# Lightning attention into an MLP: batch 1's scores ahead of the first MLP1 pair in wave 0, and masks ahead of batch 1's casts in wave 1

## Chip, cores and metric

The kernel runs on one core of a Trainium2 chip. The metric is the device time of one execution in microseconds. Before the change, five runs took 210.27 to 211.86 us, with a median of 211.44 us.

## What is computed

The reference takes q, k and v in float32, each of 4 batches, 8 heads, 768 positions and 64 channels, and one decay factor lam per head. Attention is linear: it goes through blocks of 64 positions and keeps a 64 x 64 state per head. Its result, tokens by (heads x channels) = 3072 x 512, goes through an MLP of 512 to 2048 to 512 with the activation h * sigmoid(1.702 h).

```python
for b in range(nb):
    sl = slice(b * block, (b + 1) * block)
    qb, kb, vb = (q[:, :, sl], k[:, :, sl], v[:, :, sl])
    intra = np.einsum('bhic,bhjc->bhij', qb, kb) * Dmask[None]
    intra = np.einsum('bhij,bhjd->bhid', intra, vb)
    inter = np.einsum('bhid,bhde->bhie', qb * lam_pow[None], kv_state)
    out[:, :, sl] = intra + inter
    kb_dec = kb * rev_pow[None]
    kv_state = lam_block[None, :, None, None] * kv_state + np.einsum('bhsd,bhse->bhde', kb_dec, vb)
...
h = x @ w_in
g = h * (1.0 / (1.0 + np.exp(-1.702 * h)))
return (g @ w_out).astype(np.float32)
```

## The kernel before

**Waves.** The work is cut into 6 waves of 512 tokens. Waves 0 and 1 (w < ND) are special: each takes two batches (wave 0 batches 0 and 1, wave 1 batches 2 and 3) with their first 256 positions; within such a wave the two batches are "batch 0" and "batch 1", the argument c. Waves 2 to 5 take 128 positions of all four batches. A wave is attention, which ends in a tile xT (channels by tokens, bf16), then MLP1 and MLP2. Attention of wave w+1 is placed among the MLP instructions of wave w.

**Attention of waves 0 and 1.** For each batch c, in this order:

- do_cast (L195) multiplies k or q by powers of lam and writes bf16: four instructions of 128 x 256 (L204). cast_v (L225) turns v to bf16, in two copies. These are the only readers of the loaded float32 tiles kf, qf and vf.
- turn_pe (L234) transposes the cast tile with eight TensorE transposes into PSUM (ps_t, L240) and copies the result to SBUF (kT, qT); the copy is by ScalarE (act_copy, L223) or VectorE (dve_copy, L220).
- d_one (L282) computes the state of the first 128 positions into PSUM (ps_kv, L277) and copies it to kv_sb on ScalarE (L285). In wave 1, start (L510) also keeps a float32 copy of it, `half`, on ScalarE (L513).
- d_scores (L253), twice: 16 matmuls each (L261), and two VectorE multiplications by the mask (sm, L265).
- d_even (L296) puts half of the state's share of the output into a PSUM tile (ps_o, L291) and lets ScalarE copy one column to `seen` (L299).
- end (L518) runs d_out (L301, masks by v, L309, and the other half of the state's share), d_state for the next positions, and the copies of the two output tiles to xT (d_x, L318), the first on ScalarE, the second on VectorE. It also writes the new state (L525 or L527).

**MLP.** mlp1 (L384) makes one 128-channel chunk of the hidden layer for all 512 tokens: 4 matmuls (L390) and a GELU on ScalarE (L392). mlp1_half (L394) makes two chunks for the 256 tokens of one batch: 8 matmuls (L402) and one GELU (L404). It lets MLP1 begin when only one batch's xT is there. mlp2 (L408) is one quarter of the sum for 128 tokens: 4 matmuls (L414); after the last quarter VectorE copies ps_out to o_sb (L418), which is stored.

**PSUM.** All PSUM tiles come from acc (L136) with one of two tags: "a" with 5 buffers, and "mm" with 3. MLP tiles ps_h and ps_out are in "mm", attention's are in "a" unless a tag is given.

**Order.** The schedule is written out by hand (manual_schedule): each engine runs its instructions in the order in which the program issues them. Wave 0's attention is a straight list (L455 to L508), with fill matmuls on zeros (L143) in the gaps. After that the MLP steps of all waves make a list main, and attention's steps are a list side of pairs (position, step). Before main step i, all side steps with a position of at most i are issued (L560). Wave 0 has main steps 0 to 30: three half steps, 12 MLP1 steps, then MLP2 from 15 on, first three token groups (0, 1, 2) side by side (15 to 26, whose last quarters are 24, 25 and 26), then group 3 (27 to 30). Wave 1 starts at 31 with eight half steps (31 to 38) and goes on with MLP1 at 39.

**Queues.** Loads of q, k and v and stores go through SyncE's queue; w_in and w_out go through GpSimd's. gate_pool (L448) makes GpSimd wait for a loaded tile by copying one element of it, so that the weights start behind it; gate_sync (L451) holds the loads of wave 1 until w_out's chunk 1 is there. Waves 2 to 5 transpose k and q by DMA (L247).

Of the kernel before, what the change touches and what calls it, by code (L numbers as in the profile page):

```python
# [24 lines left out]
def kernel(  # L25
# [13 lines left out]
    nc = tc.nc  # L39
    f32 = mybir.dt.float32  # L40
    bf16 = mybir.dt.bfloat16
    B, H, S, D = q.shape
    P = 128
    NP = H // 2
# [9 lines left out]
    EXP = mybir.ActivationFunctionType.Exp  # L54
# [10 lines left out]
    work = ctx.enter_context(tc.tile_pool(name="work", bufs=2))  # L65
# [5 lines left out]
    HF = 2  # L71
    HD = H * D

    loaded = {}
# [36 lines left out]
    A, Z = slice(0, 64), slice(64, P)  # L111
# [15 lines left out]
    i_k = const.tile([P, 1], f32)  # L127
    iota(i_k, [[0, 1]], P - 1, -1)
    i_q = const.tile([P, 1], f32)
# [9 lines left out]
    def fill(n, new=None):  # L139
        if new:  # L140
            fill_ps[0] = acc("ps_fill", shape=[P, W], tag=new)
        for _ in range(n):
            nc.tensor.matmul(fill_ps[0], zero[:, 0:P], zero, start=True, stop=True)  # L143
# [7 lines left out]
    def mk_pow(x, scale):  # L151
        nc.scalar.activation(x, ln_lam, EXP, scale=scale)
# [5 lines left out]
            mk_pow(x[:, :, a], i[:, a : a + 1])  # L158
    k_pow = const.tile([P, 2, H], f32)
    q_pow = const.tile([P, 2, H], f32)  # L160
    for x, i in ((k_pow, i_k), (q_pow, i_q)):
        nc.scalar.activation(x, ln_lam.unsqueeze(1).to_broadcast([P, 2, H]), EXP, scale=i)
    inv_pow = const.tile([P, H], f32)
    mk_pow(inv_pow, -1.0 * P)
    blk_pow = const.tile([P, NP], f32)
    for j, rows in enumerate((A, Z)):
        nc.scalar.activation(blk_pow[rows].rearrange("p (r i) -> p r i", i=2),
                             ln_lam[rows].rearrange("p (r j i) -> p r j i", i=2, j=2)[:, :, j, :], EXP, scale=1.0 * P)
    warm = const.tile([P, 1], f32)

    v_sb = [const.tile([P, B, H, D], bf16, name=f"v_sb{i}") for i in range(2)]
# [99 lines left out]
    def d_state(w, c, t, bs):  # L271
        ks, vt = cast[w, c, "k"], v_sb[w % 2]
        for p in range(NP):
            for a in range(2):
                for j, js in enumerate((A, Z)):
                    h, n0 = 4 * (p // 2) + 2 * j + p % 2, p * P + j * D
                    nc.tensor.matmul(t[js, p, :], ks[bs, a, n0 : n0 + D], vt[bs, 2 * c + a, h, :],  # L277
                                     start=((bs is A or (w, c) in kept) and p + a == 0), stop=(a == 1), skip_group_check=True)
# [3 lines left out]
    def d_one(w, c, tag="a"):  # L282
        states[w, c] = t = acc("ps_kv", shape=[P, NP, D], tag=tag)
        d_state(w, c, t, A)
        nc.scalar.copy(kv_sb[1][:, 2 * w + c], t)  # L285

    def d_inter(w, c, t, j, first):
        js, b = (A, Z)[j], 2 * w + c
# [7 lines left out]
    def d_even(w, c, tag="a"):  # L296
        whole[w, c] = acc("ps_o", tag=tag)
        d_inter(w, c, whole[w, c], 0, True)
        nc.scalar.copy(seen, whole[w, c][:, 0, 0:1])  # L299
# [18 lines left out]
    def d_x(w, c, i, t, copy):  # L318
        n0 = (2 * c + i) * P
        copy(xT[w][:, :, n0 : n0 + P], t)  # L320
# [73 lines left out]
    def mlp1_half(w, c, fc):  # L394
        if w not in g_of:
            g_of[w] = gp.tile([P, FFC, W], bf16, tag="g", name="g_sb")
        cols = slice(c * W // 2, (c + 1) * W // 2)
        h = acc("ps_h", shape=[P, 2, W // 2], tag="mm")
        for u in range(2):
            j, i = w_in_of[fc + u]  # L400
            for kc in range(KC):
                nc.tensor.matmul(h[:, u, :], w_in_sb[j][:, kc, i * P : (i + 1) * P], xT[w][:, kc, cols],  # L402
                                 start=(kc == 0), stop=(kc == KC - 1))
        nc.scalar.activation(g_of[w][:, fc : fc + 2, cols], h, GELU)  # L404
# [43 lines left out]
    def gate_pool(x):  # L448
        nc.gpsimd.tensor_copy(behind_q, x)
# [2 lines left out]
        nc.sync.dma_start(out=behind, in_=x)  # L452

    with tc.manual_schedule():
        nc.scalar.activation(warm, q_pow[:, 0, 0:1], GELU)  # L455
        fill(5)
        for g in range(2):
            do_cast(0, 0, "k", nc.vector, g)
            turn_pe(0, 0, "k", act_copy, g)
            fill(2)  # L460
        for g in range(2):
            do_cast(0, 0, "q", nc.vector, g)
            turn_pe(0, 0, "q", act_copy, g)
            fill(2 - 2 * g)
        gate_pool(loaded[0, 0, "v"][0:1, 0, 0:1])
        load_w_in(0)
        cast_v(0, 0, (act_copy, act_copy))
        d_scores(0, 0, 0)
        fill(1)
        d_scores(0, 0, 1)  # L470
        fill(3)
        for g in range(2):
            do_cast(0, 1, "k", nc.gpsimd, g)
        for j in (1, 2):
            load_w_in(j)
        d_one(0, 0, "mm")
        fill(1, "a")
        oa, oz = d_out(0, 0, ("mm", "mm"))
        nc.scalar.copy(seen, oz[:, 3, P - 1 : P])
        d_state(0, 0, states[0, 0], Z)  # L480
        fill(1)
        d_inter(0, 0, oz, 0, False)
        d_x(0, 0, 0, oa, act_copy)
        d_x(0, 0, 1, oz, act_copy)
        do_cast(0, 1, "q", nc.vector, 0)
        do_cast(0, 1, "q", nc.vector, 1)
        turn_pe(0, 1, "k", dve_copy)
        dve_copy(kv_sb[0][:, 0], states[0, 0])
        turn_pe(0, 1, "q", act_copy, 0)
        fill(2, "a")  # L490
        turn_pe(0, 1, "q", act_copy, 1)
        fill(2)
        cast_v(0, 1, (act_copy, pool_copy))
        for j in range(3, len(IN_CH)):
            load_w_in(j)
        for j in range(NCH):
            load_w_out(j)
        nc.gpsimd.affine_select(mask, mask, pattern=[[0, 1], [1, P]], channel_multiplier=-1, base=0,
                                compare_op=mybir.AluOpType.is_ge, fill=0.0)
        gate_sync(w_out_sb[1][0:1, 0, 0:2])  # L500
        load(1)
        d_scores(0, 1, 0)
        mlp1_half(0, 0, 0)
        d_scores(0, 1, 1)
        d_one(0, 1)
        fill(1, "mm")
        d_even(0, 1)
        fill(1)  # L508

        def start(w, c):  # L510
            d_one(w, c)
            kept[w, c] = work.tile([P, NP, D], f32, tag="half", name="half")
            nc.scalar.copy(kept[w, c], states[w, c])  # L513
            for pp in range(2):
                d_scores(w, c, pp)
            d_even(w, c)

        def end(w, c):  # L518
            oa, oz = d_out(w, c)
            t = acc("ps_kv", shape=[P, NP, D]) if w else states[w, c]  # L520
            d_state(w, c, t, Z)
            d_x(w, c, 0, oa, act_copy)
            d_x(w, c, 1, oz, dve_copy)
            if w:
                nc.vector.tensor_tensor(kv_sb[0][:, 2 * w + c], kept[w, c], t, op=ADD)  # L525
            else:
                nc.scalar.copy(kv_sb[0][:, 2 * w + c], t)  # L527

        def stores():
            for f in late:  # L530
                f()

        side, main = [(0, (end, 0, 1))], []
        for w in range(NW):
            n = len(main)
            main += mlp_items(w)
            e = len(main)
            x = w + 1
            if x < ND:
                for c in range(HF):  # L540
                    t, d = n + 24 + 5 * c, n + 19 + 7.5 * c
                    side += [(d, (do_cast, x, c, "k", nc.vector)), (d + 1 + 0.5 * c, (do_cast, x, c, "q", nc.vector)),
                             (d, (cast_v, x, c)),
                             (t, (turn_pe, x, c, "k", act_copy)),
                             (t + 1.5 + 0.5 * c, (turn_pe, x, c, "q", (act_copy, dve_copy)[c])),
                             (t + 3, (start, x, c)), (t + 6 - c, (end, x, c))]
            elif x < NW:
                for c in range(HF):
                    tk, tq = (n + 2.1 + 2 * c, n + 4 + c) if x == ND else (n + 4 + 2 * c, n + 5 + 2 * c)
                    side += [(tk, (do_cast, x, c, "k", nc.vector)), (tk, (turn_dma, x, c, "k")),  # L550
                             (tq, (do_cast, x, c, "q", nc.vector)), (tq, (turn_dma, x, c, "q")),
                             (n + 10 + 2 * c, (cast_v, x, c))]
                if x == ND:
                    side += [(n + 7, (stores,))]
                t = n + 16
                side += [(t, (n_two, x, 0)), (t + 4, (n_two, x, 1)), (t + 9, (n_rest, x))]
            if w + 2 < NW:
                side += [(n + (12 if w else 20), (load, w + 2))]
        side.sort(key=lambda x: x[0])
        for i, (f, *a) in enumerate(main):  # L560
            while side and side[0][0] <= i:
                _, (g, *b) = side.pop(0)
                g(*b)
            f(*a)
# [30 lines left out]
```

## Time and profile before

One execution was profiled. All times below are of it, unless said otherwise; starts count from the start of the span.

| what | value |
|---|---|
| median of five runs | 211.44 us (210.27 to 211.86) |
| profiled execution | 211.44 us |
| its span | 209.7 us |
| mean granted TensorE clock | 0.997 |
| TensorE busy, until 58 us / whole span | 54.72 / 203.0 us |
| VectorE, ScalarE, GpSimd busy | 90.5, 83.7, 24.6 us |
| first MLP2 matmul of wave 0 | 31.91 us |
| first full MLP1 matmul of wave 1 | 61.27 us |

The timeline gives, for a run of like instructions on an engine, the start, the length in us, the engine (PE is TensorE's matmuls, PEld its weight loads, DVE VectorE, ACT ScalarE, POOL GpSimd, SPq SyncE's DMA issues), the line, the operation, its output and inputs, the shape and the count; brackets give the idle time before the first of them and what ended it. The length of a TensorE run includes the modelled tail of its last matmul, so the prediction works with starts. The list of waits gives who waited for whom, the total in us, the number of times and the longest.

### The profile page before, as it was taken

The numbers are of one execution on the slowest core, as the hardware profiler recorded it, in microseconds if no ns is written. First come the engines' busy times: TensorE is split into PE (matmuls) and PEld (weight loads), VectorE is DVE, ScalarE is ACT, GpSimd is POOL, SyncE is SP. The second block draws the span as 40 slices with busy tenths as digits, with TensorE's granted clock in tenths as the row PEclk, the third lists the DMA queues.
The fourth block names the chain that finished last, engine by engine and source line by source line (L and its number), as shares of the span: only waits on it lengthen the run. The fifth ranks groups of instructions, "written<-read, shape, count | busy, mean of one in ns | idle before, by whom it ended". The sixth has DMA issues, their size and how long they took to land.

```text
span 209.7 us, 4320 instructions
## 1 busy us (share of the span) xinstructions
PE 203.0 (97%) x1837; PEld 105.8 (50%) x1837; DVE 90.5 (43%) x156; ACT 83.7 (40%) x153; POOL 24.6 (12%) x43
## 2 busy tenths in 40 slices
PE   7999999989899999999999999999999999999993
PEld 2567544556674455444455444464444454444463
DVE  1785000689990654650754730744720741100121
ACT  5965661134556103366102366012466021565000
POOL 4594000230220000300012000021000000000000
PEclk9999999999999999999999999999999999999998
DMA  5999999999849899989994379991370021100112
GB/s 168 335 229 203 194 205 285 303 289 216 191 109 164 193 250 221 240 186 161 239 239 141 101 174 209 221 269 55 98 158 0 20 84 50 50 0 3 50 54 96
DMA packets 87640, 33.82 MB, mean 161 GB/s; under 512 B 67398, under 2 KB 84678, under 8 KB 87622
## 3 DMA queue, kind: packets, MB, share of 16 engines
q1 hardware_dynamic: 82868, 29.37, 56.8%
q0 software_dynamic: 4752, 4.19, 12.7%
q8 instruction: 14, 0.23, 0.4%
q14 instruction: 4, 0.03, 0.0%
q10 hardware_dynamic: 2, 0.00, 0.0%
HBM read 27.26 MB, written 6.29 MB: 160 GB/s over the span
## 4 chain that ended last, share of the span: by engine, by line
PE 71%; DVE 0%; issue 0%
PE ps_out L414 34%; PE ps_h L390 30%; PE ps_s L328 2%; PE ps_o L378 2%; PE ps_h L402 2%; PE ps_o L365 1%; PE ps_kv L352 1%; DVE o_sb L418 0%
## 5 line engine op out<-in xcount | busy, mean ns | idle before, releaser
L414 PE MATMUL ps_out<-w_out,g_sb 128*128 128x512 bf16 (+2 forms) x416 | 86.2, 363 | 0.0
L390 PE MATMUL ps_h<-xT,w_in 128*128 128x512 bf16 x336 | 73.5, 379 | 0.0
L392 ACT ACTIVATE g_sb<-ps_h 128x512 bf16<-128x512 f32 x84 | 50.2, 597 | 45.2 <-PE ps_h L390 45.2
L414 PEld LDWEIGHTS <-g_sb 128*128 128x128 bf16 x416 | 38.1, 98 | 41.1
L390 PEld LDWEIGHTS <-w_in 128*128 128x128 bf16 x336 | 32.9, 98 | 39.2
L418 DVE COPY o_sb<-ps_out 128x512 f32<-128x512 f32 (+2 forms) x26 | 16.9, 650 | 53.6 <-PE ps_out L414 50.8
L336 DVE SCALAR_TENSOR_TENSOR sm<-ps_s,inv_pow,mask 128x512 bf16<-128x512 f32 x32 | 21.8, 743 | 31.4 <-PE ps_s L328 25.1
L217 POOL CAST v_sb<-vf 128x1024 bf16<-128x1024 f32 (+1 forms) x13 | 12.4, 961 | 112.4 <-DMA vf<-in_v_dram 100.3
L382 ACT CAST xT<-ps_o 128x512 bf16<-128x512 f32 x16 | 8.2, 599 | 37.8 <-PE ps_o L378 37.8
L204 DVE TENSOR_TENSOR ks<-kf,kd_pow 128x256 bf16<-128x256 f32 x12 | 5.1, 487 | 20.6 <-DMA kf<-in_k_dram 16.9
L402 PE MATMUL ps_h<-xT,w_in 128*128 128x256 bf16 x96 | 11.5, 273 | 0.8 <-DVE xT L220 0.8
L211 DVE TENSOR_TENSOR ks<-kf,k_pow 128x512 bf16<-128x512 f32 x16 | 11.9, 782 | 0.0
L143 PE MATMUL ps_fill<-zero 128*128 128x512 bf16 x27 | 10.3, 477 | 1.4 <-DVE zero L113 1.4
L265 DVE TENSOR_TENSOR sm<-ps_s,mask_d 128x512 bf16<-128x512 f32 x16 | 10.0, 682 | 2.7 <-PE ps_s L261 2.7
L211 DVE TENSOR_TENSOR qs<-qf,q_pow 128x512 bf16<-128x512 f32 x16 | 11.1, 733 | 0.0
L404 ACT ACTIVATE g_sb<-ps_h 128x512 bf16<-128x512 f32 x12 | 7.2, 597 | 7.4 <-PE ps_h L402 7.4
L402 PEld LDWEIGHTS <-w_in 128*128 128x128 bf16 x96 | 8.9, 98 | 2.4 <-DVE xT L220 1.1
L356 DVE SCALAR_TENSOR_TENSOR kv<-kv,blk_pow,ps_kv 128x256 bf16<-128x256 bf16 x12 | 5.0, 475 | 6.0 <-PE ps_kv L352 6.0
L223 ACT COPY kT<-ps_t 128x512 bf16<-128x512 bf16 (+1 forms) x4 | 3.1, 795 | 10.2 <-PE ps_t L240 10.2
L204 DVE TENSOR_TENSOR qs<-qf,qd_pow 128x256 bf16<-128x256 f32 x16 | 6.2, 451 | 0.1
L328 PEld LDWEIGHTS <-kT 64*128 64x128 bf16 x128 | 3.6, 94 | 3.4 <-issue 3.4
L328 PE MATMUL ps_s<-qT,kT 64*128 64x128 bf16 x128 | 5.0, 217 | 0.0
(64 smaller groups left out, 84.7 us busy)
## 6 DMA issues: line engine op xcount, KB each, us to landing
vf<-in_v_dram SPq DMA_DIRECT2D x11, 512.0 KB, 6.5
kf<-in_k_dram SPq DMA_DIRECT2D x10, 512.0 KB, 5.8
qf<-in_q_dram SPq DMA_DIRECT2D x10, 512.0 KB, 6.6
out_dram<-o_sb SPq DMA_DIRECT2D x15, 256.0 KB, 2.0
out_dram<-o_sb SPq DMA_DIRECT2D x17, 128.0 KB, 2.4
w_out<-in_moe_w_out_dram POOLq DMA_DIRECT2D x4, 512.0 KB, 15.1
w_in<-in_moe_w_in_dram POOLq DMA_DIRECT2D x3, 512.0 KB, 8.8
kf<-in_k_dram SPq DMA_DIRECT2D x4, 256.0 KB, 3.1
```

Of the source, the lines that this page charges most:

```text
L143: nc.tensor.matmul(fill_ps[0], zero[:, 0:P], zero, start=True, stop=True)
L204: eng.tensor_tensor(x.rearrange("p a (r i j d) -> p r j i a d", i=2, j=2, d=D)[:, R, j], f[:, h].rearrange("p i (a d) -> p i a d", a=2), p ...
L211: eng.tensor_tensor(x.rearrange("p b (r i j d) -> p j (b r) i d", i=2, j=2, d=D)[:, j], f.rearrange("p h (a d) -> p (h a) d", a=2).rearran ...
L217: nc.gpsimd.tensor_copy(out, in_)
L265: nc.vector.tensor_tensor(sm.rearrange("p i a s -> p i (a s)"), s2[h].rearrange("p (i a) s -> p i (a s)", i=2), mask_d.rearrange("p o a b ...
L328: nc.tensor.matmul(s2[h][:, b, :], kT[hs, (b % 2) * NP + p, :], qT[hs, (b % 2) * NP + p, :], start=True, stop=True)
L336: nc.vector.scalar_tensor_tensor(sm, s, inv_pow[:, n : n + 1], mask.to_broadcast([P, B, P]), op0=MUL, op1=MUL)
L390: nc.tensor.matmul(h, w_in_sb[j][:, kc, i * P : (i + 1) * P], xT[w][:, kc, :], start=(kc == 0), stop=(kc == KC - 1))
L392: nc.scalar.activation(g_of[w][:, fc, :], h, GELU)
L402: nc.tensor.matmul(h[:, u, :], w_in_sb[j][:, kc, i * P : (i + 1) * P], xT[w][:, kc, cols], start=(kc == 0), stop=(kc == KC - 1))
L414: nc.tensor.matmul(ps_out, g_of[w][:, fc, g * P : (g + 1) * P], w_out_sb[j][:, fc % CW, c0:c1], start=(fc == 0), stop=(fc == FFC - 1))
L418: nc.vector.tensor_copy(o, ps_out)
```

## The change

- The five ScalarE instructions that make k_pow, q_pow, inv_pow and blk_pow are issued inside the hand-written schedule, behind kd_pow and qd_pow.
- GpSimd's gate ahead of the first w_in chunk waits for the second half of q (heads 4 to 7) of batch 0, no longer for the first half of v.
- In wave 0 the first MLP1 half step (two chunks, 8 matmuls) moves from between batch 1's two d_scores to behind d_even, and one fill goes.
- The copies of d_one are a function of their own, d_keep; in wave 1, batch 1's d_one and d_keep move into the end of batch 0.
- In wave 1 batch 0's steps are placed earlier (k's transposes before step 22, no longer 24; q's 24, no longer 26; start 25, no longer 27; end 29, no longer 30), and batch 1's casts come behind batch 0's masks: k on GpSimd (24), q on VectorE (26). Both batches' v is cast on ScalarE (20 and 27), no longer on GpSimd.
- Batch 0's d_even takes a PSUM buffer of tag "mm"; batch 1's qT copy and the second copy to its xT go from VectorE to ScalarE.
- From wave 2 on, v is cast on VectorE, no longer on GpSimd.

```diff
--- before.py
+++ after.py
@@ -158,14 +158,8 @@
             mk_pow(x[:, :, a], i[:, a : a + 1])
     k_pow = const.tile([P, 2, H], f32)
     q_pow = const.tile([P, 2, H], f32)
-    for x, i in ((k_pow, i_k), (q_pow, i_q)):
-        nc.scalar.activation(x, ln_lam.unsqueeze(1).to_broadcast([P, 2, H]), EXP, scale=i)
     inv_pow = const.tile([P, H], f32)
-    mk_pow(inv_pow, -1.0 * P)
     blk_pow = const.tile([P, NP], f32)
-    for j, rows in enumerate((A, Z)):
-        nc.scalar.activation(blk_pow[rows].rearrange("p (r i) -> p r i", i=2),
-                             ln_lam[rows].rearrange("p (r j i) -> p r j i", i=2, j=2)[:, :, j, :], EXP, scale=1.0 * P)
     warm = const.tile([P, 1], f32)
 
     v_sb = [const.tile([P, B, H, D], bf16, name=f"v_sb{i}") for i in range(2)]
@@ -282,7 +276,12 @@
     def d_one(w, c, tag="a"):
         states[w, c] = t = acc("ps_kv", shape=[P, NP, D], tag=tag)
         d_state(w, c, t, A)
-        nc.scalar.copy(kv_sb[1][:, 2 * w + c], t)
+
+    def d_keep(w, c):
+        nc.scalar.copy(kv_sb[1][:, 2 * w + c], states[w, c])
+        if w:
+            kept[w, c] = work.tile([P, NP, D], f32, tag="half", name="half")
+            nc.scalar.copy(kept[w, c], states[w, c])
 
     def d_inter(w, c, t, j, first):
         js, b = (A, Z)[j], 2 * w + c
@@ -452,6 +451,12 @@
         nc.sync.dma_start(out=behind, in_=x)
 
     with tc.manual_schedule():
+        for x, i in ((k_pow, i_k), (q_pow, i_q)):
+            nc.scalar.activation(x, ln_lam.unsqueeze(1).to_broadcast([P, 2, H]), EXP, scale=i)
+        mk_pow(inv_pow, -1.0 * P)
+        for j, rows in enumerate((A, Z)):
+            nc.scalar.activation(blk_pow[rows].rearrange("p (r i) -> p r i", i=2),
+                                 ln_lam[rows].rearrange("p (r j i) -> p r j i", i=2, j=2)[:, :, j, :], EXP, scale=1.0 * P)
         nc.scalar.activation(warm, q_pow[:, 0, 0:1], GELU)
         fill(5)
         for g in range(2):
@@ -462,7 +467,7 @@
             do_cast(0, 0, "q", nc.vector, g)
             turn_pe(0, 0, "q", act_copy, g)
             fill(2 - 2 * g)
-        gate_pool(loaded[0, 0, "v"][0:1, 0, 0:1])
+        gate_pool(loaded[0, 0, "q"][0:1, 4, 0:1])
         load_w_in(0)
         cast_v(0, 0, (act_copy, act_copy))
         d_scores(0, 0, 0)
@@ -474,6 +479,7 @@
         for j in (1, 2):
             load_w_in(j)
         d_one(0, 0, "mm")
+        d_keep(0, 0)
         fill(1, "a")
         oa, oz = d_out(0, 0, ("mm", "mm"))
         nc.scalar.copy(seen, oz[:, 3, P - 1 : P])
@@ -500,31 +506,35 @@
         gate_sync(w_out_sb[1][0:1, 0, 0:2])
         load(1)
         d_scores(0, 1, 0)
-        mlp1_half(0, 0, 0)
         d_scores(0, 1, 1)
         d_one(0, 1)
+        d_keep(0, 1)
         fill(1, "mm")
         d_even(0, 1)
-        fill(1)
+        mlp1_half(0, 0, 0)
 
         def start(w, c):
-            d_one(w, c)
-            kept[w, c] = work.tile([P, NP, D], f32, tag="half", name="half")
-            nc.scalar.copy(kept[w, c], states[w, c])
+            if c == 0:
+                d_one(w, c)
+                d_keep(w, c)
             for pp in range(2):
                 d_scores(w, c, pp)
-            d_even(w, c)
+            d_even(w, c, ("mm", "a")[c])
 
         def end(w, c):
             oa, oz = d_out(w, c)
             t = acc("ps_kv", shape=[P, NP, D]) if w else states[w, c]
             d_state(w, c, t, Z)
+            if w and c == 0:
+                d_one(w, 1)
             d_x(w, c, 0, oa, act_copy)
-            d_x(w, c, 1, oz, dve_copy)
+            d_x(w, c, 1, oz, act_copy if w and c else dve_copy)
             if w:
                 nc.vector.tensor_tensor(kv_sb[0][:, 2 * w + c], kept[w, c], t, op=ADD)
             else:
                 nc.scalar.copy(kv_sb[0][:, 2 * w + c], t)
+            if w and c == 0:
+                d_keep(w, 1)
 
         def stores():
             for f in late:
@@ -537,19 +547,20 @@
             e = len(main)
             x = w + 1
             if x < ND:
-                for c in range(HF):
-                    t, d = n + 24 + 5 * c, n + 19 + 7.5 * c
-                    side += [(d, (do_cast, x, c, "k", nc.vector)), (d + 1 + 0.5 * c, (do_cast, x, c, "q", nc.vector)),
-                             (d, (cast_v, x, c)),
-                             (t, (turn_pe, x, c, "k", act_copy)),
-                             (t + 1.5 + 0.5 * c, (turn_pe, x, c, "q", (act_copy, dve_copy)[c])),
-                             (t + 3, (start, x, c)), (t + 6 - c, (end, x, c))]
+                for c, (k_at, q_at, v_at, k_turn, q_turn, s_at, e_at) in enumerate(
+                        ((19, 20, 20, 22, 23.5, 25, 28.5), (24, 26, 26.5, 28, 30.5, 32, 34))):
+                    side += [(n + k_at, (do_cast, x, c, "k", (nc.vector, nc.gpsimd)[c])),
+                             (n + q_at, (do_cast, x, c, "q", nc.vector)),
+                             (n + v_at, (cast_v, x, c, (act_copy, act_copy))),
+                             (n + k_turn, (turn_pe, x, c, "k", act_copy)),
+                             (n + q_turn, (turn_pe, x, c, "q", act_copy)),
+                             (n + s_at, (start, x, c)), (n + e_at, (end, x, c))]
             elif x < NW:
                 for c in range(HF):
                     tk, tq = (n + 2.1 + 2 * c, n + 4 + c) if x == ND else (n + 4 + 2 * c, n + 5 + 2 * c)
                     side += [(tk, (do_cast, x, c, "k", nc.vector)), (tk, (turn_dma, x, c, "k")),
                              (tq, (do_cast, x, c, "q", nc.vector)), (tq, (turn_dma, x, c, "q")),
-                             (n + 10 + 2 * c, (cast_v, x, c))]
+                             (n + 10 + 2 * c, (cast_v, x, c, (dve_copy,)))]
                 if x == ND:
                     side += [(n + 7, (stores,))]
                 t = n + 16
```

## The prediction

> **What bounds the kernel now.** I read the page first, then the chain that ended last, then who waited for whom between 30 and 62 us, then the timeline there. The page's first row:
>
> ```profile
> PE 203.0 (97%) x1837; PEld 105.8 (50%) x1837; DVE 90.5 (43%) x156; ACT 83.7 (40%) x153; POOL 24.6 (12%) x43
> ```
>
> The chain in order of time begins so, and nothing but PE follows until the last 0.3 us:
>
> ```profile
> 57.72 0.05 issue
> 57.77 3.67 PE ps_h L402 x32
> 61.44 6.91 PE ps_h L390 x32
> ```
>
> From 57.77 us on TensorE never waits, so no edit of later waves can gain, and a gain must come from before that point. What TensorE waited for from 30 to 62 us (total, times, longest):
>
> ```profile
> PE ps_h L402 <- DVE xT L220: 0.8, 1, 0.8
> PE ps_t L240 <- DVE sm L265: 0.3, 1, 0.3
> PE ps_o L291 <- ACT half L513: 0.2, 1, 0.2
> ```
>
> The timeline there (start, us long, engine, operation):
>
> ```profile
> 39.50 1.17 POOL L217 CAST v_sb<-vf 128x512 bf16<-128x512 f32 x2 [21.33 <-DMA vf<-in_v_dram]
> 40.33 1.01 ACT L223 COPY kT<-ps_t 128x1024 bf16<-128x1024 bf16 x1 [7.62 <-PE ps_t L240]
> 42.05 0.69 DVE L418 COPY o_sb<-ps_out 128x512 f32<-128x512 f32 x1 [0.17 <-PE ps_out L414]
> 42.50 1.01 ACT L223 COPY qT<-ps_t 128x1024 bf16<-128x1024 bf16 x1 [1.16 <-PE ps_t L240]
> 43.56 0.64 PE L261 MATMUL ps_s<-qT,kT 64*64 64x128 bf16 x32
> 43.97 2.25 DVE L204 TENSOR_TENSOR ks<-kf,kd_pow 128x256 bf16<-128x256 f32 x4
> 46.14 2.47 DVE L265 TENSOR_TENSOR sm<-ps_s,mask_d 128x512 bf16<-128x512 f32 x4
> 46.87 0.61 PE L240 MATMUL ps_t<-ident,ks 128*128 128x128 bf16 x8 [0.31 <-DVE sm L265]
> 57.03 0.68 DVE L220 CAST xT<-ps_o 128x512 bf16<-128x512 f32 x1
> ```
>
> Two things matter. The masks, ready to go at 44.0, run at 46.14 behind batch 1's k casts on VectorE. And TensorE waits for a mask at 46.87 not because it needs it, but because its new PSUM tile (tag "a", 5 buffers) takes the buffer of the first score tile; the wait on `half` is of this kind too. So buffers are reused strictly in turn.
>
> With starts of TensorE operations I sum its idle time in wave 1's attention, steps too small for the waits list included: 0.3 at 44.4, 0.5 at 46.87, 0.25 at 52.13, 0.2 at 52.88, 1.0 at 57.77: 2.2 us. That and some 0.5 us in wave 0 (the starts between 14.93 and 18.92 against the durations below) is all there is: 1.3% at the very most.
>
> **Start and wave 0.** The moved powers are the same five ScalarE instructions in another order. ScalarE runs without a gap from 3.83 to 10.41, its first kT copy at 7.26, so VectorE's casts may start 0.5 sooner (kd_pow comes first), but they then wait for ScalarE: 0 (0.1 gain at most). The gate on GpSimd waits for q's second half in place of v's first. v landed at 2.96 + 4.4 = 7.36; q's issue at 2.4, with a landing between 3.9 and 4.5 us as its neighbours, gives 6.3 to 6.9. So w_in's first chunk is issued some 0.8 us sooner, into DMA queues already full (345 GB/s at 9 to 10 us). It can delay batch 1's k (landing 8.9, read by GpSimd at 9.03) by up to 0.8 x half the rate = 0.4, and GpSimd's k casts end at 11.75 instead of 11.35; the transposes want them at 13.07: hidden. Later weights queue behind each other up to 34 us whatever the issue time: 0, bounds -0.3 to +0.4 for wave 1's loads.
>
> In wave 0 the MLP1 pair (0.98 us) goes behind d_even and one fill goes (0.22). ScalarE's state copy, at 16.96 behind the pair's GELU, moves to about 16.2, so d_even's wait (17.07 to 17.39) goes. What is late next:
>
> ```profile
> 15.39 2.62 DVE L265 TENSOR_TENSOR sm<-ps_s,mask_d 128x512 bf16<-128x512 f32 x4 [0.64 <-PE ps_s L261]
> 17.94 0.69 PE L309 MATMUL ps_o<-sm,v_sb 64*64 64x128 bf16 x32
> ```
>
> The masks still end at 18.01 and d_out's last quarter needs them. I walk d_scores 14.93, second scores 15.25 (second qT copy ends 15.19), d_one 15.78 (ScalarE's v cast ends 15.71), d_even 16.7, pair to 17.85, d_out to 18.36 instead of 18.43: 0.07 gained.
>
> **Wave 1, walked.** Durations: one MLP2 step (4 L414) 0.863 ((39.68-31.91)/9); 8 transposes 0.45; d_one 0.30; scores 0.55; d_even 0.23; d_out 0.5, then 0.11 and d_state 0.35; half MLP1 step 0.875 (57.77 to 61.27, by 4); 0.1 more on going to half-size tiles (42.30 to 43.26). ScalarE: two v casts 1.14 (row at 9.27), kT and qT copies 1.01. VectorE: masks 2.48 from 0.46 after the scores begin (52.13, 52.59), o_sb copy 0.69. A copy's end reaches TensorE 0.05 later (43.51, 43.56); transposes reach ScalarE after 0.65 (39.68, 40.33).
>
> Step 15 at 31.84. k's transposes before step 22 at 37.88 (its casts end at 37.84, as now), q's before 24 at 40.06, d_one at 41.47 to 41.77. Now the new wait. ScalarE takes v's cast before the kT copy in its in-order queue, and v lands late (KB each, us from issue to landing, one issue at 31.62):
>
> ```profile
> vf<-in_v_dram SPq DMA_DIRECT2D x1, 512.0 KB, 7.8
> ```
>
> 39.42. Casts to 40.6, kT to 41.55, qT to 42.5, scores at 42.55: TensorE waits 0.78, and 1.0 us is still gained on the old 43.56. Masks 43.01 to 45.49. d_even is now in tag "mm" (3 buffers) between ps_out of token groups 2 and 3, so group 3's ps_out reuses group 1's buffer, whose o_sb copy is behind the masks: 45.42 to 46.11. TensorE, through steps 25 and 26 at 45.06, waits to 46.17: 1.11. Queued behind it is everything on TensorE. Before, this copy ran at 42.05 and no L414 matmul waited in the trace, so the cost is bounded by 0 and 1.11; I take the upper end, because the "a" buffers show the reuse in turn twice. The Trainium skill's "Perfetto Trace Analysis" (Optimizing Tensor Performance, Matmuls) has groups rotate through PSUM banks so that the evacuation of one lies beside the next one's matmuls; here the rotation is kept but one more tile enters it. By the row of before (no wait) the sum would be 1.1 better, by the rule's condition broken it is as walked.
>
> On: step 27 to 47.03, k's transposes to 47.48, step 28, end of batch 0 from 48.44 to 49.40, d_one of batch 1 to 49.70 (its old wait on `half` goes), steps 29, 30 to 51.43, q's transposes to 51.88, half step 31 to 52.86; qT copy 52.08 to 53.09, scores 53.14 (wait 0.28), d_even to 53.92, half steps to 55.77, d_out to 56.27 (masks end 56.08), state to 56.73, step 34 to 57.61. xT's two copies on ScalarE end at 57.66: 57.68, wait 0.07 in place of 1.0. Then 3.50 to step 39: 61.18 against 61.27 now. Wave 0's 0.07 is lost in the wait for v.
>
> **What lies off the path.** Batch 1's k casts on GpSimd: the row of wave 0 has 604 ns x 4 (2.32 us) against 418 ns on VectorE. The Trainium skill's "GPSIMD Engine Reference" (4.1 Engine selection) speaks against it: two-input elementwise work is about twice as slow there. k lands between v at 39.42 and q at 42.4; by the row the cast ends at 41.8 to 44.8, by the rule (2 x 1.43) at 42.3 to 45.3; its transposes come at 47.03. Both give 0. v's casts on VectorE from wave 2 on: no row casts SBUF to SBUF there; between 0.69 (1024 elements, L220) and 1.36 (twice L211's 0.68 for 512) each, nearer the second, since it reads f32 from SBUF too. They fall at 63 to 65.6, where VectorE idles 6.28 us before 68.77; later waves have it at 49% (80 to 110 us). Zero; without that cover up to 2.7 us a wave would stand ahead of masks. Wave 2's casts start 1.1 us later behind batch 1's masks, but without GpSimd's v casts beside them 2.12 falls to 1.28; the SyncE transposes and loads behind them keep some 3 us to the scores at 68.34.
>
> **Sum.** Stalls after 0.78+1.11+0.28+0.07 = 2.24 for 2.2 before: the old waits go, two new ones take their place. Difference -0.1 us. The profiled execution took 211.44 with a span of 209.7 (1.7 around it), equal to the median: 211.3.
>
> **Rivals.** *Stalls only change places*, 0.60: 211.3, own range 210.6 to 212.1 (v's landing +-0.3, durations +-0.4). *A new wait is not there*, 0.22: if group 3 needn't wait for group 1's copy, 1.1 less: 210.2; if v lands by 38.6, the first wait goes, 0.8 less: 210.5; with both 209.4. For it: no L414 wait now; against: reuse in turn, full queues up to v. I give it 210.3. *Slower: v later*, 0.18. v to casts, kT, qT, scores, masks, o_sb copy and ps_out is one chain without slack, so each 0.1 us of v is 0.1 us of time. The earlier w_in in front of wave 0's loads holds GpSimd's casts and so every weight behind them, w_out's chunk 1 and the gate of wave 1's loads (29.75) among these. It decides from a landing of 40.6 (1.2 later); at 40.7 it gives 212.6. Against it: 1.3 us is three times what I bound. That the edits don't do what they say isn't likely: program order is plain in each engine's rows.
>
> 0.5% (1.06 us) is about what can be told from no change. Faster by more 0.22, within 0.60, slower 0.18. The range takes the nearer part of both neighbours: 210.2 to 212.5.
>
> **What would show it.** Right: scores of batch 0 at 42.5 with TensorE waiting for ScalarE's qT; masks at 43.0; a new wait of ps_out L414 on o_sb L418 near 46; xT's wait at 57.8 under 0.2; L390 starting near 61.2. Wrong: no L414 wait, v's cast on ScalarE not near 39.5, a wait of ps_t on GpSimd's k cast, or any TensorE wait after 62.

## The result: 0.63% slower, and the profile after

The changed kernel took 211.91 us (median of 38 runs, 210.70 to 214.36) against 210.61 us for the kernel before (75 runs, 209.87 to 211.86): ratio 1.0063, 95% interval 1.0049 to 1.0077. It is slower by 1.3 us, where no change was forecast. Both the lowest time (0.83 us up) and the width of the times grew. Two of the 38 runs (214.08 and 214.36 us, at a granted clock of 0.992) are slow ones, and such runs are left out of all ratios here, though not of the medians.

The profiled execution of the changed kernel took 213.01 us with a span of 211.3. Its page has these rows for TensorE's work and for the chain that ended last. DMA and SyncE's queue now have a share of the chain, which before was TensorE alone:

```profile
PE 202.8 (96%) x1836; PEld 105.7 (50%) x1836; DVE 89.5 (42%) x158; ACT 87.2 (41%) x159; POOL 15.2 (7%) x35
...
PE 75%; DMA 14%; SPq 4%; ACT 2%; DVE 1%; POOL 1%; issue 1%; DVEq 0%
```

What TensorE waited for between 30 and 64 us (total, times, longest); lines have moved, so that L413 is mlp2's matmul, L255 the scores, L234 the transposes:

```profile
PE ps_out L413 <- DVE o_sb L417: 1.0, 1, 1.0
PE ps_s L255 <- ACT qT L217: 1.0, 2, 0.8
PE ps_t L234 <- DVE ks L198: 0.5, 2, 0.3
```

The two new waits of the prediction are there, near the sizes it gave (0.78 and 1.11). The third row was not forecast: k's transposes wait for VectorE's casts. The old waits on xT, on a mask and on `half` are gone. The timeline shows the same chain, but late:

```profile
16.47 0.62 ACT L217 CAST v_sb<-vf 128x512 bf16<-128x512 f32 x1 [1.17 <-DMA vf<-in_v_dram]
17.14 0.44 PE L271 MATMUL ps_kv<-v_sb,ks 64*64 64x64 bf16 x16 [1.37 <-ACT v_sb L217]
...
38.83 1.43 DVE L198 TENSOR_TENSOR ks<-kf,kd_pow 128x256 bf16<-128x256 f32 x4 [18.02 <-DMA kf<-in_k_dram]
39.65 0.40 PE L234 MATMUL ps_t<-ident,ks 128*128 128x128 bf16 x4 [0.26 <-DVE ks L198]
40.31 0.40 PE L234 MATMUL ps_t<-ident,ks 128*128 128x128 bf16 x4 [0.27 <-DVE ks L198]
...
41.88 1.14 ACT L217 CAST v_sb<-vf 128x512 bf16<-128x512 f32 x2 [7.91 <-DMA vf<-in_v_dram]
42.93 1.00 ACT L217 COPY kT<-ps_t 128x1024 bf16<-128x1024 bf16 x1
...
44.90 0.64 PE L255 MATMUL ps_s<-qT,kT 64*64 64x128 bf16 x32 [0.78 <-ACT qT L217]
45.35 2.48 DVE L259 TENSOR_TENSOR sm<-ps_s,mask_d 128x512 bf16<-128x512 f32 x4 [0.88 <-PE ps_s L255]
47.76 0.68 DVE L417 COPY o_sb<-ps_out 128x512 f32<-128x512 f32 x1
48.49 1.02 PE L413 MATMUL ps_out<-w_out,g_sb 128*128 128x512 bf16 x4 [1.01 <-DVE o_sb L417]
```

Wave 1's v is cast at 41.88, not 39.5; every step after it is 2.3 to 2.4 us later than walked (scores 44.90 for 42.55, masks 45.35 for 43.01, ps_out 48.49 for 46.17). In wave 0, v of batch 1 is late as well, and TensorE waits 1.37 us for its cast. So TensorE is late before it comes to v of wave 1: the first MLP2 matmul starts at 33.18 us (31.84 in the walk), k's transposes at 39.65 (37.88 in the walk). Without the 0.78 us for v the scores would still have started at 44.12. The loads are late together, not that v alone: k's first cast starts at 38.83 us, where it started at 36.41 before.

The chain that ended last, in order of time, shows how a late v in wave 0 reaches wave 1:

```profile
8.60 7.86 DMA vf<-in_v_dram
16.51 0.61 POOL v_sb L211
17.12 1.44 POOL w_in L177 x2
18.55 0.72 POOL w_out L181
19.27 12.87 DMA w_out<-in_moe_w_out_dram
32.16 0.77 SPq L451
...
34.03 7.83 DMA vf<-in_v_dram
41.88 1.14 ACT v_sb L217 x2
```

GpSimd casts half of batch 1's v ahead of its issues of the rest of w_in and of w_out; w_out's chunk 1 opens SyncE's gate (L451), and wave 1's loads start behind that. So the question was not whether the walk was right, but why the loads were late.

### The profile page after: what moved, and what is told of

Its sections match the earlier page's. It is cut to its first block, busy times and chain, and to the rows that moved or that the text cites. A ratio compares the mean times of both kernels' runs of the same rounds, so it can differ in the third digit from the quotient of the medians.

```text
span 211.3 us, 4305 instructions
## 1 busy us (share of the span) xinstructions
PE 202.8 (96%) x1836; PEld 105.7 (50%) x1836; DVE 89.5 (42%) x158; ACT 87.2 (41%) x159; POOL 15.2 (7%) x35
## 4 chain that ended last, share of the span: by engine, by line
PE 75%; DMA 14%; SPq 4%; ACT 2%; DVE 1%; POOL 1%; issue 1%; DVEq 0%
PE ps_out L413 35%; PE ps_h L389 29%; DMA vf<-in_v_dram 7%; DMA w_out<-in_moe_w_out_dram 6%; SPq L81 4%; PE ps_h L401 3%; PE ps_s L327 2%; PE ps_o L377 2%; PE ps_o L364 1%; ACT qT L217 1%; DVE sm L259 1%; PE ps_kv L351 1%; POOL w_in L177 1%; PE ps_o L308 1%; ACT v_sb L217 1%
## 5 line engine op out<-in xcount | busy, mean ns | idle before, releaser
L413 PE MATMUL ps_out<-w_out,g_sb 128*128 128x512 bf16 (+2 forms) x416 | 86.4, 363 | 1.0 <-DVE o_sb L417 1.0
L413 PEld LDWEIGHTS <-g_sb 128*128 128x128 bf16 x416 | 38.2, 98 | 42.2 <-issue 1.3
L198 DVE TENSOR_TENSOR ks<-kf,kd_pow 128x256 bf16<-128x256 f32 x8 | 2.9, 421 | 21.3 <-DMA kf<-in_k_dram 18.0
L205 DVE TENSOR_TENSOR qs<-qf,q_pow 128x512 bf16<-128x512 f32 x16 | 10.3, 684 | 0.0
L205 DVE TENSOR_TENSOR ks<-kf,k_pow 128x512 bf16<-128x512 f32 x16 | 10.3, 683 | 0.0
L217 ACT CAST v_sb<-vf 128x512 bf16<-128x512 f32 x7 | 4.0, 617 | 9.6 <-DMA vf<-in_v_dram 9.6
L198 POOL TENSOR_TENSOR ks<-kf,kd_pow 128x256 bf16<-128x256 f32 x8 | 4.7, 607 | 22.7 <-DMA kf<-in_k_dram 21.6
L217 ACT COPY qT<-ps_t 128x512 bf16<-128x512 bf16 (+1 forms) x6 | 4.4, 728 | 2.0 <-PE ps_t L234 1.8
```

The lines of the kernel that those rows point to most:

```text
L198: eng.tensor_tensor(x.rearrange("p a (r i j d) -> p r j i a d", i=2, j=2, d=D)[:, R, j], f[:, h].rearrange("p i (a d) -> p i a d", a=2), p ...
L205: eng.tensor_tensor(x.rearrange("p b (r i j d) -> p j (b r) i d", i=2, j=2, d=D)[:, j], f.rearrange("p h (a d) -> p (h a) d", a=2).rearran ...
L217: nc.scalar.copy(out, in_)
L413: nc.tensor.matmul(ps_out, g_of[w][:, fc, g * P : (g + 1) * P], w_out_sb[j][:, fc % CW, c0:c1], start=(fc == 0), stop=(fc == FFC - 1))
```

## The experiments

Each ratio is to runs of the kernel before taken beside that kernel; their median went from 210.20 to 210.66 us, so ratios compare better than medians.

| kernel | runs | lowest us | median us | ratio to before (95%) |
|---|---|---|---|---|
| 1 wave-1 part only | 18 | 210.73 | 211.43 | 1.0058 (1.0035 to 1.0081) |
| 2 changed, gate on v | 6 | 212.04 | 213.15 | 1.0122 (1.0074 to 1.0170) |
| 3 changed, powers back | 20 | 210.66 | 211.97 | 1.0073 (1.0050 to 1.0095) |
| 4 before, gate on q | 22 | 209.87 | 210.00 | 0.9983 (0.9966 to 1.0000) |
| 5 changed, batch 0's v on GpSimd | 22 | 209.79 | 211.04 | 1.0006 (0.9989 to 1.0023) |
| 6 changed, d_even in "a" | 22 | 209.51 | 210.62 | 0.9997 (0.9974 to 1.0021) |
| 7 changed, loads sooner | 6 | 211.80 | 212.49 | 1.0085 (1.0053 to 1.0117) |
| 8 before, batch 1's v on ScalarE | 22 | 209.81 | 209.87 | 0.9970 (0.9954 to 0.9985) |
| 9 both waits taken away (5 and 6) | 22 | 209.04 | 210.08 | 0.9970 (0.9950 to 0.9989) |
| 10 old order, waits taken away | 24 | 209.69 | 209.73 | 0.9969 (0.9954 to 0.9985) |
| 11 wave-0 part only | 14 | 209.70 | 210.53 | 0.9991 (0.9964 to 1.0019) |
| 12 as 9, old wave 0 | 22 | 209.17 | 210.26 | 0.9975 (0.9953 to 0.9997) |
| 13 as 12, one step later | 12 | 209.13 | 209.17 | 0.9937 (0.9916 to 0.9957) |
| 14 before, profiled again | 1 | 210.37 | | |

**1 to 4: which part, and is it the gate or the powers?** Kernel 1 is the kernel before with the wave-1 part (and the later v casts) alone.

> Only the wave-1 part and the later v casts; start and wave 0 as before. Theory A (the gate lets the first w_in chunk in front of batch 1's loads, so v of wave 0 and all weights are late): v of wave 1 lands near 39.4 again, scores of batch 0 near 42.5, ratio to before 0.997 to 1.002. Theory B (the moved powers start VectorE's casts earlier and SyncE's issues of the loads then take longer): the same here. Theory C (loads land later in some executions whatever the kernel, and only wave 1's new order without slack shows it): still 1.004 to 1.007.

Kernel 2 is the changed kernel with one line back:

```diff
-        gate_pool(loaded[0, 0, "q"][0:1, 4, 0:1])
+        gate_pool(loaded[0, 0, "v"][0:1, 0, 0:1])
```

> The changed kernel with GpSimd's gate back on v. Theory A: batch 1's v lands near 12.6 in place of 16.5, ratio to before 0.997 to 1.002. Theories B and C: as the changed kernel, 1.005 to 1.008, v near 16.

Kernel 3 puts the five powers back where they were:

```diff
     with tc.manual_schedule():
-        for x, i in ((k_pow, i_k), (q_pow, i_q)):
-            nc.scalar.activation(x, ...)
-        mk_pow(inv_pow, -1.0 * P)
...
```

> The changed kernel with the powers back in their old order. Theory B: SyncE's issue of k of batch 1 takes 1.8 us again in place of 2.7, v of batch 1 lands near 13, ratio 0.997 to 1.002. Theories A and C: 1.005 to 1.008.

Kernel 4 has nothing but the gate's line of the change.

> The kernel before with the gate on q's second half alone. Theory A: v of batch 1 later than 14, the loads of wave 1 1 to 2 us later, but the time only 0 to 0.5% longer, since the old wave-1 order has some 2.6 us between v's cast and its first reader. Theories B and C: no change, 0.998 to 1.002.

The wave-1 part alone gives the whole loss (1.0058). Theories A and B fall: with the gate back the changed kernel is still slower than before (1.0122), the gate alone costs nothing (0.9983), and with the powers back the loss stays (1.0073). Kernel 3's profile happens to be one in which wave 1's loads come as early as in the first profile of before, and it is a test of the walk:

```profile
36.48 1.44 DVE L204 TENSOR_TENSOR ks<-kf,kd_pow 128x256 bf16<-128x256 f32 x4 [17.05 <-DMA kf<-in_k_dram]
...
39.54 1.14 ACT L223 CAST v_sb<-vf 128x512 bf16<-128x512 f32 x2 [6.94 <-DMA vf<-in_v_dram]
...
42.55 0.64 PE L261 MATMUL ps_s<-qT,kT 64*64 64x128 bf16 x32 [0.69 <-ACT qT L223]
43.01 2.48 DVE L265 TENSOR_TENSOR sm<-ps_s,mask_d 128x512 bf16<-128x512 f32 x4 [0.79 <-PE ps_s L261]
...
46.15 1.02 PE L419 MATMUL ps_out<-w_out,g_sb 128*128 128x512 bf16 x4 [1.01 <-DVE o_sb L423]
...
60.92 3.40 PE L395 MATMUL ps_h<-xT,w_in 128*128 128x512 bf16 x14
```

Walked were 42.55, 43.01, 46.17 and 61.18. This execution took 210.69 us, 0.75 less than the profiled 211.44 of before. Only 0.35 of this lies ahead of wave 1's full MLP1 (60.92 against 61.27). The other 0.4 lies at the very end, behind VectorE's last output copy: from the start of that MLP1 to the end of the copy both take 145.4 us. All ten profiles of kernels with the change's wave 1 and its later v casts have this gain (the time less that start is 149.73 to 149.77 us), and the six others don't (150.11 to 150.18). Which edit brings it was not tested.

In the other profiles the loads come later. The five profiles that have the changed wave 1 with both new waits give:

| kernel | k's cast on VectorE starts, us | v's cast on ScalarE starts, us | scores start, us | time of that execution, us |
|---|---|---|---|---|
| 3 | 36.48 | 39.54 | 42.55 | 210.69 |
| 1 | 36.74 | 39.80 | 42.81 | 210.94 |
| 2 | 38.18 | 41.24 | 44.25 | 212.36 |
| 7 | 38.32 | 41.38 | 44.39 | 212.50 |
| changed | 38.83 | 41.88 | 44.90 | 213.01 |

From first to last v is 2.34 us later and the time 2.32 us longer, and the three between lie on that line within 0.03. But k is later by the same amount: v follows it by 3.05 or 3.06 us in all five, and the scores by 6.07. So this table can't tell a chain through v from one through k. The kernels below that take v out of ScalarE's way can: in three of them (5, 12 and 13) TensorE waits for k's casts, and the scores start 5.16 us behind the first of these. So k has no slack either. The lateness that k and v share goes into the time in full, and v's place ahead of kT costs 0.9 us on top (6.07 less 5.16).

**5 and 6: one wait each.** Kernel 5 takes v out of the way of ScalarE's copies, kernel 6 frees ps_out from the masks:

```diff
-                             (n + v_at, (cast_v, x, c, (act_copy, act_copy))),
+                             (n + v_at, (cast_v, x, c, ((pool_copy, pool_copy), (act_copy, act_copy))[c])),
```

> The changed kernel with wave 1's batch 0 v cast on GpSimd again, so that ScalarE's kT and qT copies no longer queue behind v. Theory D (the loss is two new waits, qT behind v 0.8 us and more when v lands late, and ps_out behind the masks 1.0 us): the scores start near 41.8, the qT wait is under 0.1, the ps_out wait stays at 1.0; 0.8 us faster than the changed kernel at its best (210.7 to 209.9) and its spread to higher times shrinks; ratio to before 0.996 to 1.001. Theory E (the loss is the extra work on ScalarE and GpSimd, not the waits): 1.005.

```diff
-            d_even(w, c, ("mm", "a")[c])
+            d_even(w, c)
```

> The changed kernel with batch 0's d_even in a PSUM buffer of tag a again. Theory D: no wait of ps_out on o_sb; instead d_even waits some 0.2 to 0.3 us for the copy half; at its best 0.8 us faster than the changed kernel (209.9), the spread stays as wide, since v is still ahead of kT; ratio 1.000 to 1.003. Theory E: 1.006.

Each brings the lowest time down, by 0.9 and 1.2 us from the changed kernel's 210.70; in kernel 6's profile no ps_out wait is left, in kernel 5's that wait stands at 0.9 and no qT wait of batch 0 is left. Theory E falls. In kernel 5 the spread did not shrink as expected: with v out of the way it is k's casts, just as late, that TensorE waits for (k first cast at 37.81, a wait of 0.5 us in all, scores at 42.97).

**7: loads sooner.** The gate of wave 1's loads waits for w_out's chunk 0:

```diff
-        gate_sync(w_out_sb[1][0:1, 0, 0:2])
+        gate_sync(w_out_sb[0][0:1, 0, 0:2])
```

> The changed kernel with the loads of wave 1 held only until w_out's chunk 0 is there. Theory D: v lands 1.5 to 2.4 us sooner, the qT wait goes (0.8), the ps_out wait of 1.0 stays, most of the spread goes; ratio 0.996 to 1.001, unless w_out's chunks 1 to 3 now come too late for MLP2, which would show as a wait of L413 on the DMA of w_out. Theory E: 1.006.

A miss. The first load was issued at 29.32 us (30.57 in the first profile of before), but v was cast at 41.38: it took 10.9 us from issue to landing, where it took 7.8 in the changed kernel's profile. Between 29 and 42 us GpSimd's queue still moved 1.13 MB through the same DMA engines; that this took v's share is likely, but no run separates it. The time follows k and v as in the table.

**8 and 14: was the profile of before a typical one?** Its v casts of batch 1 on GpSimd lay exactly on VectorE's k casts. Kernel 8 moves them to ScalarE, behind batch 0's scores:

```diff
-                             (d, (cast_v, x, c)),
+                             ((d, 28.2)[c], (cast_v, x, c, ((pool_copy, pool_copy), (act_copy, act_copy))[c])),
```

> The kernel before with wave 1's batch 1 v cast on ScalarE, behind batch 0's scores, so that it no longer lies beside VectorE's k cast. Theory F (in its profiled execution VectorE's k casts took 2.25 us beside GpSimd's v casts in place of 1.42, which made the 0.3 and 0.8 us waits; executions without that overlap are the fast ones): k casts 1.42 us, no xT wait, times from 209.9 up with fewer above 211, ratio 0.996 to 1.000. If those waits belong to the old order itself: ratio 1.000, xT's wait stays.

> The kernel before once more, for a second profile. Theory H: k of wave 1's batch 0 is first read later than the 36.41 us of the first profile, most likely at 37.5 to 38.3; batch 1's v then lands after VectorE's k casts, these take 1.42 in place of 2.25 us, there is no xT wait of 0.8, and the time is 209.9 to 210.4. If the first profile was typical: 36.4 again, 2.25, the wait of 0.8, 211.4.

Kernel 8 is 0.30% faster, and its times are narrow: 17 of 22 below 210.1. The second profile of the unchanged kernel (kernel 14) shows why the times of before vary. First two lines of the first profile, then kernel 14's timeline, then all its waits of TensorE from 30 to 64 us:

```profile
36.41 1.43 DVE L204 TENSOR_TENSOR ks<-kf,kd_pow 128x256 bf16<-128x256 f32 x4 [16.87 <-DMA kf<-in_k_dram]
...
43.99 1.62 POOL L217 CAST v_sb<-vf 128x512 bf16<-128x512 f32 x2 [3.32 <-DMA vf<-in_v_dram]
```

```profile
37.96 1.43 DVE L204 TENSOR_TENSOR ks<-kf,kd_pow 128x256 bf16<-128x256 f32 x4 [17.95 <-DMA kf<-in_k_dram]
...
44.44 1.42 DVE L204 TENSOR_TENSOR ks<-kf,kd_pow 128x256 bf16<-128x256 f32 x4
...
45.78 2.48 DVE L265 TENSOR_TENSOR sm<-ps_s,mask_d 128x512 bf16<-128x512 f32 x4
45.81 1.17 POOL L217 CAST v_sb<-vf 128x512 bf16<-128x512 f32 x2 [3.61 <-DMA vf<-in_v_dram]
```

```profile
PE ps_o L291 <- ACT half L513: 0.6, 2, 0.4
PE ps_out L414 <- issue: 0.2, 1, 0.2
```

k is first read at 37.96, 1.55 us later than in the first profile; batch 1's v then lands behind VectorE's k casts and beside the masks. The casts take 1.42 us where they took 2.25, the v casts 1.17 where they took 1.62, and the waits on a mask and on xT (0.3 and 0.8) are not there. The Trainium skill's "SBUF — State Buffer" (Who interferes with whom) says that a VectorE instruction with two SBUF inputs contends with a GpSimd instruction that reads SBUF, and one with at most one SBUF input, outside the modes in which VectorE takes two ports, does not. Both measurements agree: k casts (two inputs in SBUF) slow down, masks (one in PSUM) take 2.48 us beside the same v casts. So in the kernel before the later loads of kernel 14 gave the faster execution (210.37 against 211.44 us); in the changed kernel, every late load costs.

**9 and 10: both waits taken away, in the new and in the old order.** Kernel 9 is kernels 5 and 6 in one.

> The changed kernel with both mends: batch 0's v of wave 1 on GpSimd, and its d_even in a tag a buffer. Theory D: neither the qT wait (over 0.1) nor the ps_out wait; at its best 208.8 to 209.2, 1.5 to 1.9 us below the changed kernel's 210.7; ratio 0.993 to 0.998. If the two mends don't add, because what was hidden behind the one wait comes out (the transposes waiting for k's casts, d_one waiting for v): 209.5 at its best, ratio 0.997 to 1.001.

Its profile's waits from 0 to 66 us (a wait at the very start left out) are:

```profile
PE ps_o L290 <- ACT half L284: 0.2, 1, 0.2
PE ps_s L255 <- ACT qT L217: 0.2, 1, 0.2
```

The mends bring 1.66 us of the 2.1 that they brought one by one: 209.04 at the lowest against the changed kernel's 210.70, and 0.30% faster than before. Kernel 10 keeps the old positions:

```diff
-                    t, d = n + 24 + 5 * c, n + 19 + 7.5 * c
...
+                        ((19, 20, 20, 24, 25.5, 27, 30), (26.5, 28, 28.2, 29, 31, 32, 34))):
...
-            d_even(w, c)
+            d_even(w, c, ("mm", "a")[c])
```

> The old order of waves 0 and 1 with only those edits that take a wait away: batch 1's v on ScalarE behind batch 0's scores, d_even of batch 0 in tag mm (here the o_sb copies stand ahead of the masks), batch 1's d_one in the end of batch 0, the gate on q. Theory D and F: the 0.6 us of waits on half go and no ps_out wait comes; 209.2 at its best, tight, ratio 0.993 to 0.996. If the mm buffer costs a ps_out wait in this order too: 209.8 or more.

Half a miss: no ps_out wait came, so tag "mm" costs nothing where the o_sb copies stand ahead of the masks, but the 0.6 us did not become time. In its profile (210.73 us, near the top of its runs, which go from 209.69 to 210.93) a wait of 0.3 on qT's VectorE copy, which d_one had covered before, and 0.2 on xT stand in their place.

**11 to 13: where does the rest of the spread come from?** Kernel 11 is the kernel before with the start and wave 0 of the change, kernel 12 is kernel 9 with the old order in wave 0.

> The kernel before with the start and wave 0 of the change alone (powers, gate, d_one and d_even ahead of the first MLP1 pair). Theory G (d_one no longer has the pair ahead of it, so that TensorE waits for v of batch 1 when that lands late, at 16 us as in the changed kernel's profile): best 209.8, median 0.3 to 0.8 higher than that of the gate alone (210.0), ratio 1.000 to 1.004. Without it: 0.997 to 0.999 as the gate alone.

> The changed kernel with both mends in wave 1 and with the old order in wave 0 (first MLP1 pair between the two d_scores, the fill back). Theory G (the rest of the spread comes from d_one in wave 0, which has lost the pair's 1 us of cover for a late v): best 209.1 to 209.2, as without the old order, but a median within 0.5 of the best in place of 1.0; ratio 0.993 to 0.996. If the spread comes from wave 1's earlier readers of k, q and v: best 209.1, median near 210.1 still, ratio 0.996 to 0.998.

Kernel 11's profile has the wait (1.14 us of d_one on v's cast), but over its runs it can't be told from before (0.9991). Kernel 12's median stays 1.1 above its lowest: wave 0 is not the main source. In its profile k of wave 1 is first cast at 37.49, and its transposes, at step 22, wait 0.5 us. Kernel 13 moves batch 0's transposes, start and end by one step:

```diff
-                        ((19, 20, 20, 22, 23.5, 25, 28.5), (24, 26, 26.5, 28, 30.5, 32, 34))):
+                        ((19, 20, 20, 23, 24.5, 26, 29.5), (24, 26, 26.5, 29, 30.5, 32, 34))):
```

> The twelfth kernel with batch 0's transposes, start and end one MLP2 step (0.86 us) later. Theory H (the loads of wave 1 land anywhere in some 2.4 us, and the change put their readers where only the earliest landing is in time): 0.86 us of slack for k takes most of the late executions; best 209.2 to 209.5, median within 0.4 of the best, ratio 0.993 to 0.996. If the spread has another source: median about 1.0 above the best as before, ratio 0.997 to 0.999.

All its times lie between 209.13 and 209.74, 0.63% below before (0.9916 to 0.9957). It beats both kernels: it has the change's order, without the two waits, and one step of slack for the loads; 0.4 us of its gain is the one at the very end. Its profile's wait on k's casts is 0.3 us with k first cast at 38.07, later than in kernel 12. Its lowest time is that of kernel 12 (209.13 and 209.17), its median 1.1 us lower: the step takes away the spread.

## Why the prediction was wrong

What came was the effect of the rival "slower: v later", to which the prediction gave 0.18: 0.1 us of time for 0.1 us of lateness, as in the table, though k is as late as v and would have been waited for without it. Its path (GpSimd's cast of v, the weights behind it, w_out's chunk 1, the gate) is the chain that the changed kernel's profile shows; its cause (the new gate) is not. That 211.91 us still lies in the range given, 210.2 to 212.5, is luck: the late loads cost some 1.2 us (211.91 against kernel 3's 210.69), and the walk ended 0.6 us above what kernel 3 took. The steps, in order:

- *"39.42. Casts to 40.6"* and *"its casts end at 37.84, as now"*. The step that failed: the landings of v and k were taken from one profile, v's with 0.3 us to either side, k's with nothing. In the sixteen profiles of this case the first v cast of wave 1 starts between 39.50 and 41.88 us, in twelve of them at 40.57 or later. The 39.50 of the profile of before was the earliest of all. With a v of 40.6 to 41.4 the walk gives 212.4 to 213.2 in place of 211.3; in the changed kernel's profile, v at 41.88 gave 213.01.
- *"2.24 for 2.2 before"*. The second failure, of the same root. 1.0 us (xT) and 0.5 us (mask) of it belong to an execution in which early loads put v's casts on k's. The second profile of before has 0.6 us of waits on `half` in this stretch and 210.37 us. So what the change could win in such an execution was a third of what was counted; the base was 0.83 us too high (211.44 against the median of 75 runs, 210.61). Of the 1.4 us between the forecast difference (-0.1) and the measured one (1.3) this is more than half.
- *The walk itself* was right: in kernel 3, with the loads as assumed, its marks were met within 0.3 us, the ps_out wait with 1.01 for 1.11. The upper end for that wait was the right choice.
- *"no edit of later waves can gain"*: too strong a conclusion from the sight that TensorE never waits there: 0.4 us was won behind the last copy, a term that the prediction put at nothing.
- *The reason given for a late v* (w_in ahead of it through the new gate) was wrong: kernels 2 and 4. In the unchanged kernel, with the old gate, v can be as late: in kernel 14 GpSimd's cast in wave 0 is at 15.97 (12.84 in the first profile) and the first v cast of wave 1 at 41.04.
- *Wave 0, 0.07 gained*: with early loads it was 0.11 (the 24 half-step matmuls from 18.81 in kernel 3, 18.92 before). With a late v it costs up to the 1.37 us of the changed kernel's profile; the pair ahead of d_one had covered that. The prediction took v's landing there from one profile as well (5.1 us from issue to landing, where the changed kernel's took 7.9).
- *Off the path*: right. GpSimd's k casts took 2.33 us from 43.44 and were wanted at 49.35. v's casts on VectorE took 1.28 us for two, just below the lower bound of 0.69 each, and hid. No cost of the powers showed (kernel 3).

What makes the loads of the first 16 us, and with them all weights and the loads of wave 1, land up to 2.4 us apart from one execution to the next was not settled. Batch 1's v in wave 0, one load of 512 KB, took 5.1 us from issue to landing in the first profile of before and 8.1 in kernel 14's, the same kernel, so the change of gate or powers isn't needed for it. What follows from a late v there is seen more plainly: in the five profiles in which GpSimd casts it by 14.61 us, the gate of wave 1's loads opens by 30.15; in the ten others with that gate, at 30.62 or later. No run took that cast out of GpSimd's queue, which would have tested the link.

## What to carry to other kernels

A reader of a load that is placed where one profile shows the load just landed has no slack, and the median pays for the spread of the landing: one step later (0.86 us) was worth more here than the earlier start. Before costing waits from a profile, compare its own time with many runs: 211.44 us was the median of the first five, but 66 of 75 runs were faster, and the profile showed waits that a second one doesn't have. And a copy that waits for a load should not stand in an in-order queue ahead of copies that need nothing from it (0.9 us here), nor a new tile enter a rotation of PSUM buffers whose next release stands behind long work (1.0 us here).

## What was not expected of the hardware

Early loads made the kernel before slower: k casts of 1.42 us took 2.25 beside GpSimd's v casts, and 211.44 us stood against 210.37 with the later loads. Starting wave 1's loads 1.2 us sooner (kernel 7) did not make v land sooner (cast at 41.38, against 39.5 to 41.9 elsewhere). And on GpSimd the two-input k cast took 604 to 607 ns against VectorE's 418, 1.45 times as long (in chains of four 2.33 against 1.43 us, 1.6 times), where the rule cited in the prediction has about two.
